# A transformer block's backward: nine buffers for the DMA-transposed ds tiles, two of their own for the one that TensorE transposes, six for the exps

## The chip, the cores and the metric

The kernel runs on one core of a Trainium2 chip. The metric is the device time of one execution in microseconds (us); the number that counts is the median over several executions. A profile is one execution, recorded instruction by instruction.

## What is computed

One transformer block with attention and a gated feed-forward network side by side, forward and backward in one launch. The sizes are S = 2048 tokens, D = 448, H = 16 heads of 28, F = 1792, all in bf16.

```python
def _fwd_reference(A_x, A_wqkv, A_wo, B_x, B_w_gate, B_w_up, B_w_down):
    ...
        scores = jnp.einsum("bhqd,bhkd->bhqk", q, k) * (Dh ** -0.5)
        p = _softmax(scores, axis=-1)
        o = jnp.einsum("bhqk,bhkd->bhqd", p, v)
        ...
        return (g * u) @ w_down
    x = A_x
    xn = _layernorm(x, axis=-1)
    return x + _A_ref(xn, A_wqkv, A_wo) + _B_ref(xn, B_w_gate, B_w_up, B_w_down)

def reference(A_x, A_wqkv, A_wo, B_w_gate, B_w_up, B_w_down, B_x, grad_out):
    ...
    _out, _vjp = jax.vjp(_f, A_x, A_wqkv, A_wo, B_w_gate, B_w_up, B_w_down)
    _grads = _vjp(grad_out)
    return (_out0, *[jnp.asarray(_g) for _g in _grads])
```

The outputs are the block's result and the gradients of the input and of the five weights.

## The kernel before

The order of all work is written out by hand; every engine runs its own list in that order, and waits are put in where a buffer or a value is not there yet. The first 610 us or so are the forward pass and the backward of the feed-forward network. What follows, up to some 1385 us, is the backward of attention, which the change touches; then a short end writes the gradient of the input.

**The loop.** The backward of attention runs 512 steps. A step is one tile of 512 keys by 128 queries for two heads; four steps with qi = 0, 1, 2, 3 are a block b of 512 queries, and there are 128 blocks. The list `steps` names the group of four heads (g), the head pair (hp), the chunk of keys (kc), the chunk of queries (qc) and qi of each step. Iteration k of the loop puts out:

- `row(k)`: on TensorE the scores of step k into PSUM banks named `sb` (L844, two heads) and the matrix that the softmax derivative needs for step k - 1 into banks named `db` (L852). Each name has three banks, and a bank holds one head, so `db` holds one and a half steps.
- `ew(k)`: on ScalarE the exponentials of step k out of `sb` into the SBUF tile `e_sb` (L868), and on VectorE ds of step k - 1 as the product of `db` and `e_sb` into the tile `ds_sb` (L874).
- For qi = 0, 1 and 2, straight after ds, a DMA transpose issued from SyncE (SP), which writes `ds_sb` transposed into the tile `dsT` of the block (L861, function `dst_dma`). Loads of later data (L801) stand in the same SP list, spread over the iterations by a planner (`drip` and `drop`).
- In iterations with k % 4 = 3, `tr_unit(b)` for b = (k - 7) / 4: the tile with qi = 3 is transposed by eight TensorE transposes (L929) and copied into `dsT` by ScalarE (L934). So the tile of step 4b + 3 is read here in iteration 4b + 7. In the very last block the tile with qi = 2 goes this way too.
- In iterations with k % 4 = 1, `kv` for the four steps of the last finished block, which reads `e_sb` (L947) and `ds_sb` (L951) on TensorE; block b is read in iteration 4b + 5. Then `dq_unit(b)` for b = (k - 13) / 4, which reads the block's whole `dsT` in sixteen matmuls (L978); block b is read in iteration 4b + 13.
- In the remaining places, pieces of other work on TensorE from a list (`stream`): the output of the feed-forward network (L1101), the gradient through gate and up (L1157) and more, each sized by the time there is.

**Buffers.** A tile name in a pool is a ring: with `bufs=8`, the ninth tile takes the place of the first and its first writer waits until all readers of that first tile are done. `ds_sb` has eight buffers and `e_sb` seven, 2 KB on each partition, in the pool `kq`. `dsT` has three, in the pool `bk`. The first three steps of the loop come before `bk` is opened; while `bk` is `None`, the transposes are kept in `pend` until it is.

**The end.** `dx_v` (L1298) and `dx_b` (L1337) take tiles of the rings `ds_sb` and `e_sb` for the last stage of the input's gradient.

Of the kernel before, what the change touches and what calls it, by code (L numbers as in the profile page):

```python
# [11 lines left out]
FP32 = mybir.dt.float32  # L12
BF16 = mybir.dt.bfloat16
# [4 lines left out]
D = 448  # L18
# [7 lines left out]
P = 128  # L26
# [79 lines left out]
def kernel(  # L106
# [465 lines left out]
    for i in range(len(chain) + LEAD):  # L572
# [4 lines left out]
        k = i - LEAD  # L577
# [117 lines left out]
    for c in range(3):  # L695
        k = 4 * c
        t = 4 * c + 4
# [35 lines left out]
    kq = None  # L733
# [87 lines left out]
    est, dss, sps, dps = {}, {}, {}, {}  # L821
# [34 lines left out]
    bk, pend = None, []  # L856

    def dst_dma(b, ds, qi):
        if qi == 0:
            dsT[b] = bk.tile([P, 4, 2, 4, P], BF16, name="dsT", bufs=3)  # L860
        SP.dma_start_transpose(out=dsT[b][:, qi].rearrange("p j kt s -> p (j kt) s"),  # L861
                               in_=ds[:].rearrange("p j k -> p (j k)"))

    def ew(k):
        if k < NB:
            est[k] = kq.tile([P, 2, 512], BF16, name="e_sb", bufs=7)
            for j in range(2):
                ACTE.activation(out=est[k][:, j], in_=sps.pop((k, j))[:], func=ACT.Exp, scale=SCALE)  # L868
        if 1 <= k <= NB:
            g, hp, kc, qc, qi = steps[k - 1]  # L870
            b = (k - 1) // 4
            ds = dss[k - 1] = kq.tile([P, 2, 512], BF16, name="ds_sb", bufs=8)
            for j in range(2):
                DVE.tensor_tensor(out=ds[:, j], in0=dps.pop((k - 1, j))[:], in1=est[k - 1][:, j], op=ALU.mult)  # L874
            if qi < 2 or qi == 2 and b < NB // 4 - 1:
                if bk is None:
                    pend.append(lambda: dst_dma(b, ds, qi))
                else:
                    dst_dma(b, ds, qi)
# [9 lines left out]
    k = n = 0  # L889
    for u in last[-5:]:  # L890
        for _ in u():
            n += 1
            if n in (8, 17, 25, 32):
                row(k)
                ew(k)
                k += 1
# [3 lines left out]
    bk = bwd.enter_context(tc.tile_pool(name="bk", bufs=2, reuse_waits="tile"))  # L900
# [393 lines left out]
    vs = {}  # L1294

    def dx_v(t):
        ps = psd.pop(t)
        vs[t] = kq.tile([P, 512], FP32, name="ds_sb", bufs=8)[:, :D]  # L1298
        dy = dy2[t // 4][:, t % 4, :] if t < 8 else dy4[:, t - 8, :]
        DVE.scalar_tensor_tensor(out=vs[t], in0=ps, scalar=rstd[:, t:t + 1], in1=dy, op0=ALU.mult, op1=ALU.add)  # L1300

    def sums(t, i):
        return sms[t - t % 2][:, i, t % 2:t % 2 + 1] if t < NT - 2 else sms[NT - 2 + i][:, t % 2:t % 2 + 1]
# [10 lines left out]
    def dx_a(t0):  # L1314
        for t in (t0, t0 + 1):
            ps = psd[t]
            sa, sb = sums(t, 0), sums(t, 1)
            if t not in EVEN:
                gs = dxs["tw"].tile([P, D], BF16, name="gs")
                ACTE.activation(out=gs[:], in_=ps, func=ACT.Identity, accum_out=sa)  # L1320
            else:
                psd[t] = dxs["g"][:, t, :]
                DVE.scalar_tensor_tensor(out=psd[t], in0=ps, scalar=1.0, in1=psd[t],
                                         op0=ALU.mult, op1=ALU.add, accum_out=sa)
            pr = dxs["tw"].tile([P, D], BF16, name="pr")
            DVE.scalar_tensor_tensor(out=pr[:], in0=psd[t], scalar=1.0, in1=xn_sp[:, t, :],
                                     op0=ALU.mult, op1=ALU.mult, accum_out=sb)
        if t0 == NT - 2:
            dx_sm(t0)
        for t in (t0, t0 + 1):  # L1330
            dx_v(t)
        if t0 < NT - 2:
            dx_sm(t0)

    def dx_b(t):
        sa, sb = sums(t, 0), sums(t, 1)
        u = kq.tile([P, 512], FP32, name="e_sb", bufs=7)[:, :D]  # L1337
        ACTE.activation(out=u, in_=xn_sp[:, t, :], func=ACT.Identity, scale=sb, bias=sa)  # L1338
        dx = dxs["tw"].tile([P, D], BF16, name="dx", bufs=4)
        (DVE if t == NT - 1 else POOL).tensor_tensor(out=dx[:], in0=u, in1=vs.pop(t), op=ALU.add)  # L1340
        SP.dma_start(out=out1_d[:, t, :], in_=dx[:])
# [3 lines left out]
    for k in range(NB + 12):  # L1345
        now = k
        if k < NB:
            g, hp, kc, qc, qi = steps[k]
# [7 lines left out]
        if k <= NB:  # L1356
            if k >= K0:
                row(k)
                ew(k)
            flush(k)  # L1360
            if 2 <= k:
                drop()
# [48 lines left out]
    for t in range(4, NT + 2, 2):  # L1411
        if t < NT:
            dx_mm(t)
            dx_a(t)
        for u in range(0 if t == 4 else t - 2, t):
            dx_b(u)
        for _ in range(at.get(t, 0)):
            run(rest.pop(0))
# [33 lines left out]
```

## Time and profile before

| | us |
|---|---|
| three runs | 1420.4, 1427.53, 1424.92 |
| their median | 1424.92 |
| the profiled execution | 1428.21 |
| its span, first to last instruction | 1426.4 |
| granted TensorE clock over the span | 0.974 of full |
| VectorE, L874: 1024 products of 684 ns, busy | 645.4 |
| ScalarE, L868: 1024 exponentials of 607 ns, busy | 541.7 |
| SP queue, hardware DMA: share of the 16 DMA engines | 88.6% |

The page gives the busy time of each engine, and the granted clock and the DMA load in 40 slices. A row of a group of instructions has its line, engine, operation, tiles and count, then busy time and the mean of one, then the idle time of the engine before them and what ended it. In a timeline the first two numbers are start and length, and the bracket holds the idle time before and its releaser. A list of waits has the total, the number of times and the longest, in us. A wait is put down to the engine that came last by the profile; now and then another name stands there than the one that was waited for.

### The profile page before, as it was taken

To read this page: it belongs to the slowest core of one execution; us is meant where nothing else is said; L and a number is where in the kernel's file an instruction comes from. 1 tells how busy PE (TensorE), PEld (TensorE's weight loads), DVE (VectorE), ACT (ScalarE), POOL (GpSimd) and SP (SyncE) were. 2 spreads that over 40 slices of the span, in tenths; PEclk is the share of its full clock that TensorE was granted. 3 is DMA by queue.
4 is the path that set the end of the run, shared out by engine and by line. 5 is a ranking of instruction groups with operands and counts; after the bars stand their busy time and mean duration, and the time that the engine had idled before them with its cause. 6 is when DMAs were issued, how large, how long until landed. Compare 5 with 4: busy or idle time off the path is not lost. (4 is left out here: it accounts for less than half of the span.)

```text
span 1426.4 us, 34639 instructions
## 1 busy us (share of the span) xinstructions
PE 1326.9 (93%) x12625; PEld 559.9 (39%) x12686; DVE 1149.3 (81%) x2001; ACT 1208.3 (85%) x2190; POOL 411.3 (29%) x577
## 2 busy tenths in 40 slices
PE   5899999999999999889999999999899999999995
PEld 2333333333333333334434434444344443444443
DVE  6677757666677676478989889988799998999988
ACT  5799988989999999768978779899789897888864
POOL 6574514454344454011211212201111112020105
PEclk9999999999999999989999999999999999999998
DMA  5797957796678686699999999999999999999982
GB/s 155 178 198 174 241 117 165 185 206 154 146 177 189 149 174 158 187 232 217 206 213 221 217 222 181 214 213 223 224 192 192 214 212 227 214 186 205 197 142 61
DMA packets 681692, 270.22 MB, mean 189 GB/s; under 512 B 607402, under 2 KB 656034, under 8 KB 681522
## 3 DMA queue, kind: packets, MB, share of 16 engines
q1 hardware_dynamic: 673074, 254.78, 88.6%
q0 software_dynamic: 7040, 12.93, 4.0%
q8 instruction: 99, 1.62, 0.5%
q14 instruction: 71, 0.58, 0.1%
q10 hardware_dynamic: 1408, 0.30, 0.1%
HBM read 64.37 MB, written 59.62 MB: 87 GB/s over the span
## 5 line engine op out<-in xcount | busy, mean ns | idle before, releaser
L874 DVE TENSOR_TENSOR ds_sb<-db,e_sb 128x512 bf16<-128x512 f32 x1024 | 645.4, 684 | 65.0 <-DMA dsT<-ds_sb 16.4
L868 ACT ACTIVATE e_sb<-sb 128x512 bf16<-128x512 f32 x1024 | 541.7, 607 | 55.4 <-PE db L852 45.4
L636 ACT ACTIVATE eT<-s_w 128x1024 bf16<-128x1024 f32 x256 | 264.6, 1033 | 54.2 <-PE s_ps L633 51.8
L638 ACT ACTIVATE eT<-s_ps 128x512 bf16<-128x512 f32 x512 | 287.2, 614 | 0.0
L852 PE MATMUL db<-kd,qd 32*128 32x512 bf16 x1024 | 239.6, 387 | 17.1 <-DVE ds_sb L874 16.6
L844 PE MATMUL sb<-kd,qd 32*128 32x512 bf16 x1024 | 232.9, 386 | 8.9 <-DMA qd<-QD_d 5.3
L993 POOL TENSOR_TENSOR dq_acc<-dq_acc,dq_st 128x256 f32<-128x256 f32 x64 | 46.2, 722 | 484.7 <-ACT dq_st L991 484.7
L404 POOL TENSOR_TENSOR nn<-nn,ag 128x512 f32<-128x512 f32 x56 | 71.2, 1271 | 242.2 <-DVE ag L402 233.5
L951 PE MATMUL acc<-ds_sb,qd 128*32 128x512 bf16 x1024 | 138.9, 393 | 0.2 <-DVE ds_sb L874 0.2
L947 PE MATMUL acc<-e_sb,qd 128*32 128x512 bf16 x1024 | 138.4, 393 | 0.0
L633 PE MATMUL s_ps<-QQ,KK 32*128 32x512 bf16 x512 | 120.3, 387 | 2.2
L1157 PE MATMUL genb<-wguT,dau_c 128*128 128x448 bf16 x448 | 110.5, 357 | 0.5 <-DMA dau_c<-F_d 0.5
L633 PE MATMUL s_w<-QQ,KK 32*128 32x512 bf16 x512 | 100.7, 389 | 3.6 <-ACT eT L636 1.2
L844 PEld LDWEIGHTS <-qd 32*128 32x128 bf16 x1024 | 48.5, 91 | 135.3 <-issue 114.7
L445 PE MATMUL gen<-xn_t,f_sp 128*128 128x448 bf16 x416 | 91.8, 354 | 3.2 <-DVE nn L419 1.9
L934 ACT COPY dsT<-sb 128x512 f32<-128x512 f32 x128 | 75.5, 590 | 18.1 <-PE sb L929 10.0
L445 PEld LDWEIGHTS <-f_sp 128*128 128x128 bf16 x640 | 55.7, 98 | 77.3 <-issue 32.3
L978 PE MATMUL sb<-dsT,kd 128*32 128x256 bf16 x2048 | 80.7, 279 | 0.7 <-ACT dsT L934 0.7
L929 PE MATMUL sb<-ident_bf,ds_sb 128*128 128x128 bf16 x1032 | 79.3, 220 | 1.0 <-DVE dsT L932 0.8
L929 PEld LDWEIGHTS <-ds_sb 128*128 128x128 bf16 x1032 | 67.7, 98 | 27.0 <-issue 8.3
L405 POOL TENSOR_TENSOR nn<-nn,tt 128x512 f32<-128x512 f32 x56 | 72.5, 1294 | 4.4
L475 PE MATMUL gen<-eT,VS 128*32 128x512 bf16 x1024 | 68.6, 383 | 5.3 <-ACT eT L638 2.2
(179 smaller groups left out, 1919.9 us busy)
## 6 DMA issues: line engine op xcount, KB each, us to landing
F_d<-hda SPq DMA_DIRECT2D x56, 384.0 KB
dau_c<-F_d SPq DMA_DIRECT2D x24, 512.0 KB
qd<-QD_d SPq DMA_DIRECT2D x16, 512.0 KB
kd<-KD_d SPq DMA_DIRECT2D x16, 384.0 KB
dsT<-ds_sb SPq DMA_TRANSPOSE x383
h_c<-F_d SPq DMA_DIRECT2D x8, 512.0 KB
wT_d<-wT_f SPq DMA_DIRECT2D x14, 256.0 KB
KD_d<-qk_sp SPq DMA_DIRECT2D x7, 512.0 KB
```

The costliest lines, as they stand in the source:

```text
L445: PE.matmul(ps[:, :D], lhsT=fsp[fc][:, t // 4, w, t % 4, :], rhs=rhs[:, t, :], start=(t == 0), stop=(t == NT - 1))
L633: PE.matmul(sp4[hh], lhsT=KK[g][r:r + HP, kt * P:(kt + 1) * P], rhs=QQ[g][r:r + HP, qsl], start=True, stop=True, tile_position=(r, 0))
L636: ACTE.activation(out=e2[0][:], in_=wide[:], func=ACT.Exp, scale=SCALE)
L638: ACTE.activation(out=e2[1][:, j], in_=sp4[2 + j], func=ACT.Exp, scale=SCALE)
L844: PE.matmul(s_ps[:], lhsT=qside[g, qc][r:r + HP, 0, qi * P:(qi + 1) * P], rhs=kside[g, kc][r:r + HP, 0, :], start=True, stop=True, tile_po ...
L852: PE.matmul(d_ps[:], lhsT=qside[g, qc][r:r + HP, 1, qi * P:(qi + 1) * P], rhs=kside[g, kc][r:r + HP, 1, :], start=True, stop=True, tile_po ...
L868: ACTE.activation(out=est[k][:, j], in_=sps.pop((k, j))[:], func=ACT.Exp, scale=SCALE)
L874: DVE.tensor_tensor(out=ds[:, j], in0=dps.pop((k - 1, j))[:], in1=est[k - 1][:, j], op=ALU.mult)
L929: PE.transpose(ps[:, c, :], ds[:, c // 4, (c % 4) * P:(c % 4 + 1) * P], ident_bf[:])
L947: PE.matmul(a[r:r + HP, :], lhsT=sp4[:, 1, r:r + HP], rhs=e[:, j, :], start=first, stop=last, tile_position=(0, r), skip_group_check=True)
L951: PE.matmul(a[r:r + HP, :], lhsT=sp4[:, 0, r:r + HP], rhs=ds[:, j, :], start=first, stop=last, tile_position=(0, r), skip_group_check=True)
L1157: PE.matmul(ps[:, :D], lhsT=d[:, i // 2, i % 2, tsl], rhs=dxs["w", fq][:, i // 2, i % 2, :], start=(i == 0), stop=(i == n - 1))
```

## The change

The tile of ds with qi = 3 no longer comes from the ring `ds_sb` but from a new ring `ds_pe` in the pool `bk`, which has two buffers, the pool's default. The ring `ds_sb` gets nine buffers instead of eight, the ring `e_sb` six instead of seven. So the pool `kq` has as much as before (15 tiles of these two names), and `bk` has two tiles of 2 KB on each partition more. The two other places where the rings are used (L1298 and L1337) have the new counts as well.

```diff
-            est[k] = kq.tile([P, 2, 512], BF16, name="e_sb", bufs=7)
+            est[k] = kq.tile([P, 2, 512], BF16, name="e_sb", bufs=6)
...
-            ds = dss[k - 1] = kq.tile([P, 2, 512], BF16, name="ds_sb", bufs=8)
+            by_pe = qi == 3 and bk is not None
+            ds = dss[k - 1] = (bk.tile([P, 2, 512], BF16, name="ds_pe") if by_pe else
+                               kq.tile([P, 2, 512], BF16, name="ds_sb", bufs=9))
...
-        vs[t] = kq.tile([P, 512], FP32, name="ds_sb", bufs=8)[:, :D]
+        vs[t] = kq.tile([P, 512], FP32, name="ds_sb", bufs=9)[:, :D]
...
-        u = kq.tile([P, 512], FP32, name="e_sb", bufs=7)[:, :D]
+        u = kq.tile([P, 512], FP32, name="e_sb", bufs=6)[:, :D]
```

## The prediction

> **What bounds the kernel now.** I read the page first (engines and slices), then stretches of the backward, the waits inside it, and the timeline around one wait. Columns of the stretches: start:end, length, busy time of PE, PEld, DVE, ACT and POOL, granted TensorE clock, mean share of the 16 DMA engines, GB/s.
>
> ```profile
> PE 1326.9 (93%) x12625; PEld 559.9 (39%) x12686; DVE 1149.3 (81%) x2001; ACT 1208.3 (85%) x2190; POOL 411.3 (29%) x577
> ```
> ```profile
> 720.00:750.00 30.00, 28.45 (x312) 11.69 (x311) 26.95 (x45) 22.83 (x46) 3.78 (x6) 0.94 1.20 209
> ...
> 780.00:815.00 35.00, 32.61 (x370) 14.15 (x372) 31.76 (x53) 29.20 (x59) 6.64 (x11) 0.97 1.13 215
> 815.00:835.00 20.00, 18.02 (x176) 7.22 (x169) 13.82 (x23) 12.44 (x26) 5.07 (x8) 0.80 1.12 238
> ...
> 850.00:880.00 30.00, 30.00 (x345) 13.32 (x342) 29.59 (x49) 27.69 (x56) 5.13 (x8) 1.00 1.02 187
> 1005.00:1025.00 20.00, 16.08 (x176) 6.33 (x174) 14.33 (x23) 12.57 (x26) 4.34 (x7) 0.91 1.09 221
> ...
> 1195.00:1215.00 20.00, 16.93 (x184) 6.99 (x183) 14.65 (x25) 12.84 (x27) 4.35 (x7) 0.91 1.10 221
> ```
>
> The backward (about 610 to 1385 us) is bound by TensorE: 850 to 880 shows PE at 30.00 of 30 us with full clock. Only in some stretches is PE idle, and there the clock falls too. The waits from 620 to 1385 us (us in total, times, longest) say behind whom:
>
> ```profile
> PE db L852 <- DVE ds_sb L874: 16.1, 19, 2.2
> ...
> DVE ds_sb L874 <- DMA dsT<-ds_sb: 16.4, 12, 3.5
> ```
>
> And one such wait, PE alone, SP alone, DVE alone:
>
> ```profile
> 717.94 0.39 PE L852 MATMUL db<-kd,qd 32*128 32x512 bf16 x1
> 720.49 0.55 PE L852 MATMUL db<-kd,qd 32*128 32x512 bf16 x1 [2.17 <-DVE ds_sb L874]
> ...
> 722.58 0.61 PE L844 MATMUL sb<-kd,qd 32*128 32x512 bf16 x2
> ```
> ```profile
> 712.53 5.59 SPq L861 DMA_TRANSPOSE dsT<-ds_sb  x2
> 718.16 0.60 SPq L801 DMA_DIRECT2D h_c<-F_d  x1
> 718.86 6.08 SPq L861 DMA_TRANSPOSE dsT<-ds_sb  x4
> ```
> ```profile
> 719.75 0.69 DVE L874 TENSOR_TENSOR ds_sb<-db,e_sb 128x512 bf16<-128x512 f32 x1 [2.59 <-DMA dsT<-ds_sb]
> ```
>
> The product ds (L874) cannot be written because the DMA transpose of the tile eight steps back has not landed. DVE stands for 2.59 us. The three db banks fill, PE stands for 2.17 us, and then its matmuls take 0.61 us instead of 0.39: the clock is at half for a while. SP has no hole: its transposes follow each other at 1.23 us or more.
>
> **What one such wait costs.** PE idle first. In the timeline of PE, the gaps of 0.4 us or more that end on L874 are 2.17, 1.06, 0.63, 0.63, 1.43, 1.98, 0.61, 2.22, 1.37, 1.56 and 0.40 us: 14.1 of the 16.1 us. Clock next, from the stretches above: (1 - 0.94) x 30 = 1.8, (1 - 0.97) x 35 = 1.0, 0.20 x 20 = 4.0, 0.09 x 20 = 1.8 twice: 10.4 us of full-speed time lost. What the transposes cost today is then 14.1 + 10.4 = 24.5 us.
>
> Here a rule speaks against half of that sum. The Trainium skill, page "TensorE: Matmul & The Clock Gate", section "Part 1: The HAM clock gate", has the clock fall after an idle window of about 3.4 us; no gap above is that long, so by the rule the 10.4 us would not belong to the waits, and the sum below would be -5.3 us instead of -12.3. The trace has the slow matmuls directly behind the 2.17 us gap, so I keep the 10.4 us.
>
> **The change part by part.**
>
> 1. Reuse distance of the transposed tiles. Before, all ds tiles go round eight buffers: step s waits for step s - 8. Now one in four (qi = 3) has other buffers and the rest go round nine: nine tiles are three blocks of four steps, so step s waits for step s - 12. A block takes about 5.7 us, so the DMA gets one block more. All waits on L874 for a DMA should go: -24.5 us, if nothing later is late.
>
> 2. What is late next. The same transpose is read by dq_unit(b) (L978), which PE reaches in iteration 4b + 13. Tile qi = 2 is reused before in iteration 4b + 11. The distance between the two in the trace: DVE freed at 719.75, 733.76, 751.13, 774.47, 798.18 us, dq_unit of that block at 724.40, 736.87, 754.25, 777.59, 801.29 us, so 4.6, 3.1, 3.1, 3.1, 3.1 us. So the margin is 3.1 us, not a whole block. SP issues without a hole, so a queue that is late stays late until a quieter stretch: I let waits that follow each other closely add up, take 3.1 us off each cluster, and put the rest on PE at L978. The DVE idle times that end with a landing (some carry another engine's name, which was done before; I went by the landing of the tile eight steps back): 0.76 + 2.59 + 1.43 = 4.8 (705 to 734 us), 0.67 + 1.01 + 0.45 + 1.01 + 1.31 + 2.36 = 6.8 (751 to 826), 0.88 + 1.21 + 0.63 = 2.7 (930 to 985), 0.55 + 2.30 + 1.77 = 4.6 (1007 to 1020), 0.65 (1123), 3.48 (1203). Rest: 1.7 + 3.7 + 0 + 1.5 + 0 + 0.4 = 7.3 us. Bounds: 0 (the margin and idle SP time suffice) and 23.1 us (the sum of all, nothing absorbed). I take 7.3, as the waits sit in clusters with quiet between. Behind a waiting dq_unit stands all of PE's queue, the next row (L844, L852) first, then ACT and DVE.
>
> 3. Clock after those waits. Gaps of 1.06 us and less left the clock alone, gaps of 1.4 and 2 us mostly did not. Two of the new waits may be that long: 2 x 1.7 us (half of a 3.4 us slow stretch, the length between 720.5 and 724) = 3.4 us. Bounds 0 and 10.4 us.
>
> 4. Loads. At 1200.5 us PE waits 1.5 us for qd and at 988 us 0.5 us for dau_c, both behind the same SP queue. With the loop faster they come no earlier: +1.5 us, between 0 and 4 (each twice).
>
> 5. ds of qi = 3 in two buffers of its own. Freed by kv in iteration 4b + 5 and by the transposes (L929) in 4b + 7, wanted again in 4b + 12: five iterations, 7 us, of cover. Cost 0. With the cover gone it would be the 0.6 us of the eight transposes once a block, 128 x 0.6 = 77 us.
>
> 6. e_sb six instead of seven. The exp of step k needs step k - 6 read by kv and by L874. kv of a block runs in iteration 4b + 5; the earliest exp that needs it is now in 4b + 6 instead of 4b + 7. But that exp reads an sb bank whose matmul (L844) stands behind this kv in PE's queue, so it waits no longer than it does anyway. L874 of step k - 6 is covered by the three db banks, which keep PE within two steps of DVE. Cost 0; bound below 0 excluded, above it one exp pair (2 x 607 ns) a block, which the order excludes.
>
> 7. Places in memory. kq keeps its size, bk grows by two tiles and pools behind it move. The order on PE, DVE, ACT, POOL and SP is the same instruction for instruction; only waits differ. New waits on forward work: the second exp tile waits for POOL L404 and DVE L431, which last started at 580.5 and 585.3 us, against the exp at 608.19 us. Cost 0.
>
> 8. The end: the 16 tiles of L1338 go round six instead of seven buffers behind POOL L1340 (1.2 us each). POOL waits for DVE there (31.2 us), so 0; bound +1.2 us, one L1340.
>
> Sum: -24.5 + 7.3 + 3.4 + 1.5 = -12.3 us. The profiled execution took 1428.2 us (span 1426.4 and 1.8 around it): 1415.9. It lies 3.3 us above the median of the runs shown, 1424.9; I carry the difference over: 1412.6, say **1412.5 us**.
>
> **The rivals.**
>
> *All of it is won.* If the queue recovers between waits, items 2 to 4 are 0: 1424.9 - 24.5 = 1400.4 us. For it: single waits at 1123 and 1203 us are far apart. Against: SP without a hole at 706 to 725 us. Chance 0.15.
>
> *The queue is the bound.* DMA share 1.02 to 1.20 in all stretches. If the transposes come at the DMA engines' pace, all 23.1 us come back at L978, less clock loss: -24.5 + 23.1 = about 1424 us. Against: 850 to 880 us, where the DMA is as full and PE never waits. The profile's page counts 607402 of 681692 DMA packets under 512 B. Chance 0.28. The Trainium skill, page "DMA: Bandwidth & Descriptors", section "Specifications", puts the least transfer for line rate at 512 B; by it these transposes are bound by their packets, and a buffer more would win nothing.
>
> *Slower: the wait lands where it costs most.* A late ds is softened by 1.5 steps of db banks; a late dsT stops PE at once, at L978, and each stop over 1.3 us may cost a slow stretch. With all 23.1 us there and as many slow stretches as waits over 0.6 us (15 x 1.7 = 25): -24.5 + 48 = +24, 1449 us. It decides once waits plus clock at L978 pass 24.5 us. Against: the margin of 3.1 us. Chance 0.12.
>
> *It does not do what it says*: the ring of eight never held DVE, the named releaser being wrong. Then 1425 us. Against: the 2.59 us wait has nothing else to end it. Chance 0.03.
>
> **How the numbers follow.** The forecast has 0.42, its own range 1405 to 1420 us. What a measurement of this kernel can tell from no change is about 0.5%, 7 us. Faster: 0.36 of the forecast's 0.42, 0.15, and 0.05 of the queue case = 0.56. Same: 0.06 + 0.21 + 0.03 = 0.30. Slower: 0.12, and 0.02 of the queue case = 0.14. The range 1400 to 1432 us leaves out most of the slower case and some of the fullest win.
>
> **What would show it.** After: no "DVE ds_sb L874 <- DMA dsT" in the waits (item 1), a new wait of L978 for the DMA of dsT of some 7 us (item 2), granted clock 1.00 at 1005 to 1025 and 1195 to 1215 us or their like, PE's wait for L874 down from 16.1 to a few us. ACT e_sb L868 waiting for PE acc L947 would prove item 6 wrong. If L978 waits more than 20 us for the DMA, the queue was the bound and the forecast is wrong.

## The result and the profile after

The changed kernel takes 1417.45 us (median of eight runs, 1409.88 to 1419.96) against 1425.47 us for the one before (eight runs): ratio 0.9935, 95% interval 0.991 to 0.996, so 8 us less. It was measured beside its kernel before in two more sessions: 0.9944 (0.9923 to 0.9964) and 0.9898 (0.9876 to 0.9920). The profiled execution took 1417.71 us, its span is 1415.9 us. Lines below the edit have moved by two: the ds product is L876, `dq_unit`'s matmuls are L980.

The engines on the page of the changed kernel, first TensorE's row:

```profile
PE 1326.4 (94%) x12686; PEld 558.6 (39%) x12686; DVE 1147.4 (81%) x2001; ACT 1208.5 (85%) x2190; POOL 411.1 (29%) x577
```

The busy times are those of before; the span is 10.5 us shorter, and its mean granted clock is 0.978 against 0.974. The stretches of the changed kernel (columns as before):

```profile
720.00:750.00 30.00, 30.00 (x350) 13.21 (x351) 29.53 (x50) 27.64 (x56) 3.78 (x6) 1.00 1.22 198
780.00:815.00 35.00, 34.15 (x401) 14.80 (x389) 33.92 (x57) 30.97 (x62) 7.35 (x12) 1.00 1.17 223
815.00:835.00 20.00, 14.47 (x154) 5.72 (x155) 12.35 (x21) 11.60 (x24) 4.35 (x7) 0.91 1.15 239
850.00:880.00 30.00, 29.86 (x364) 13.29 (x353) 29.27 (x49) 27.28 (x56) 5.14 (x9) 1.00 1.11 202
1005.00:1025.00 20.00, 18.33 (x208) 8.00 (x206) 17.33 (x29) 17.22 (x36) 3.22 (x5) 1.00 1.15 234
1185.00:1205.00 20.00, 17.25 (x189) 7.21 (x187) 15.31 (x27) 13.46 (x28) 4.52 (x8) 0.91 1.15 225
```

At 720 to 750 us PE is now busy throughout, with full clock; before it lost 1.55 us idle and 1.8 us to the clock there. Two of these stretches are still bad, at 815 and at 1185 us. The list of PE's waits from 620 to 1385 us in the changed kernel (us in total, times, longest) says what fills them:

```profile
PE sb L980 <- DMA dsT<-ds_sb: 4.9, 4, 2.7
PE sb L844 <- DMA qd<-QD_d: 4.4, 2, 2.7
...
PE sb L844 <- DMA kd<-KD_d: 1.9, 1, 1.9
PE db L852 <- DVE ds_sb L876: 1.4, 5, 0.5
...
PE genb L1159 <- DMA dau_c<-F_d: 0.3, 1, 0.3
```

PE's wait for the ds product fell from 16.1 to 1.4 us, and the DVE's wait for the DMA of dsT is gone from the list altogether. In its place PE waits 4.9 us for dsT itself, at `dq_unit`, and 6.3 us for loads of qd and kd. All four waits for dsT lie between 773 and 825 us. The longest of them and the wait for kd behind it, then the granted clock (third number from the end) in the stretch between the two and right after the second:

```profile
817.27 0.62 PE L980 MATMUL sb<-dsT,kd 128*32 128x256 bf16 x16 [2.67 <-DMA dsT<-ds_sb]
...
829.41 0.61 PE L844 MATMUL sb<-kd,qd 32*128 32x512 bf16 x2 [1.90 <-DMA kd<-KD_d]
```
```profile
816.00:829.00 13.00, 8.88 (x102) 3.86 (x102) 7.98 (x13) 7.96 (x16) 4.35 (x7) 1.00 1.17 248
829.00:833.00 4.00, 3.59 (x24) 1.05 (x28) 2.59 (x5) 1.89 (x4) 0.00 (x0) 0.57 1.13 209
```

How one of the loads comes late, SP first, then PE:

```profile
1183.84 4.02 SPq L861 DMA_TRANSPOSE dsT<-ds_sb  x2
1187.91 1.31 SPq L801 DMA_DIRECT2D qd<-QD_d  x1
1189.31 3.99 SPq L861 DMA_TRANSPOSE dsT<-ds_sb  x2
```
```profile
1193.41 0.39 PE L844 MATMUL sb<-kd,qd 32*128 32x512 bf16 x2 [2.73 <-DMA qd<-QD_d]
```

The load is issued at 1187.91 us between transposes, PE is ready for it at 1190.68 us, and it is there at 1193.41 us.

### The profile page after: what moved, and what is told of

Same layout as the page of the kernel before. It is cut to its first block, busy times and chain, and to the rows that moved or that the text cites. A ratio compares the mean times of both kernels' runs of the same rounds, so it can differ in the third digit from the quotient of the medians.

```text
span 1415.9 us, 34707 instructions
## 1 busy us (share of the span) xinstructions
PE 1326.4 (94%) x12686; PEld 558.6 (39%) x12686; DVE 1147.4 (81%) x2001; ACT 1208.5 (85%) x2190; POOL 411.1 (29%) x577
## 5 line engine op out<-in xcount | busy, mean ns | idle before, releaser
L876 DVE TENSOR_TENSOR ds_sb<-db,e_sb 128x512 bf16<-128x512 f32 x768 | 482.0, 683 | 36.4 <-issue 13.8
L852 PE MATMUL db<-kd,qd 32*128 32x512 bf16 x1024 | 234.1, 385 | 2.9 <-DVE ds_sb L876 1.4
L876 DVE TENSOR_TENSOR ds_pe<-db,e_sb 128x512 bf16<-128x512 f32 x256 | 164.8, 686 | 19.2 <-PE db L852 10.9
L953 PE MATMUL acc<-ds_sb,qd 128*32 128x512 bf16 x768 | 108.4, 391 | 0.0
L980 PE MATMUL sb<-dsT,kd 128*32 128x256 bf16 x2048 | 80.1, 277 | 5.7 <-DMA dsT<-ds_sb 4.9
L931 PE MATMUL sb<-ident_bf,ds_pe 128*128 128x128 bf16 x1024 | 78.6, 220 | 1.0 <-DVE dsT L934 0.8
L931 PEld LDWEIGHTS <-ds_pe 128*128 128x128 bf16 x1024 | 67.3, 98 | 26.9 <-issue 8.2
```

The source lines that it names most:

```text
L852: PE.matmul(d_ps[:], lhsT=qside[g, qc][r:r + HP, 1, qi * P:(qi + 1) * P], rhs=kside[g, kc][r:r + HP, 1, :], start=True, stop=True, tile_po ...
L931: PE.transpose(ps[:, c, :], ds[:, c // 4, (c % 4) * P:(c % 4 + 1) * P], ident_bf[:])
L953: PE.matmul(a[r:r + HP, :], lhsT=sp4[:, 0, r:r + HP], rhs=ds[:, j, :], start=first, stop=last, tile_position=(0, r), skip_group_check=True)
```

## The experiments

The first three tell apart what brought the 8 us; the others ask what bounds the rest. All are compared with the kernel before on their own chip.

**Six ds_sb buffers: the distance undone, all else kept.**

```diff
-                               kq.tile([P, 2, 512], BF16, name="ds_sb", bufs=9))
+                               kq.tile([P, 2, 512], BF16, name="ds_sb", bufs=6))
```

> The changed kernel with six ds_sb buffers instead of nine: a transposed tile is reused after 8 steps again, ds_pe and the six exps stay. If the reuse distance is what brought the 8 us, the time goes back to that of before, about 1425 us, with DVE waiting at the ds product for the DMA of dsT some 15 to 25 us again. If it was that the tile of qi = 3 has buffers of its own (its place, or its leaving the ring), the time stays at about 1417 us.

Measured: 1427.11 us, ratio 1.0004 (0.998 to 1.0028). Two waits of its backward, the first on PE, the second on DVE:

```profile
PE db L852 <- DVE ds_sb L876: 16.8, 20, 2.5
```
```profile
DVE ds_sb L876 <- DMA dsT<-ds_sb: 16.4, 12, 2.7
```

Both are back at what they were before (16.1 and 16.4 us), and the whole gain is gone, although the tile of qi = 3 still has buffers of its own. So it is the reuse distance of the transposed tiles that the change lives from; the two own buffers and the six exps bring nothing without it, they make room for it.

**Eight ds_sb buffers: ten or eleven steps.**

```diff
-                               kq.tile([P, 2, 512], BF16, name="ds_sb", bufs=9))
+                               kq.tile([P, 2, 512], BF16, name="ds_sb", bufs=8))
```

> The changed kernel with eight ds_sb buffers instead of nine: the distance is 10 or 11 steps. A tile of qi = 2 would then be reused in iteration 4b + 14, after dq_unit has read its transpose in 4b + 13. If dq_unit is the next thing that a late transpose holds, the ninth buffer does nothing: 1417 us, no wait of DVE for the DMA. If the time follows the number of buffers, it lies between, about 1420 us.

Measured: 1418.56 us, ratio 0.9933 (0.9914 to 0.9953), the same as with nine. PE's and then DVE's list:

```profile
PE sb L980 <- DMA dsT<-ds_sb: 4.8, 6, 1.4
PE sb L844 <- DMA qd<-QD_d: 4.8, 2, 2.4
```
```profile
DVE ds_sb L876 <- DMA dsT<-ds_sb: 3.8, 4, 1.8
```

DVE still waits four times, 3.8 us, which the expectation did not have: the tile of qi = 0 is then reused ten steps later, in iteration 4b + 11, before `dq_unit`. No cost of it shows, and no gain of the ninth buffer; the step from 8 to 10 or 11 brings all that these intervals, some 0.2% to either side, can tell.

**Six exps, nothing else.** The kernel before with `e_sb` at six:

```diff
-            est[k] = kq.tile([P, 2, 512], BF16, name="e_sb", bufs=7)
+            est[k] = kq.tile([P, 2, 512], BF16, name="e_sb", bufs=6)
```

> The kernel before with six exps instead of seven and nothing else. If the sixth-back exp is always read before TensorE can fill the next score bank, the time is that of before, 1425 us within 0.3%, and the exps never wait for kv. If the shorter ring costs something that the net of 8 us hides, the time is some 3 us or more above before, 1428 us and more, with ScalarE waiting for kv.

Measured: 1427.7 us, ratio 0.9996 (0.9978 to 1.0013). ScalarE's longest wait in its backward is the one of before (42.8 us, 57 times), and no wait of the exps for kv is in the list:

```profile
ACT e_sb L868 <- PE db L852: 39.9, 58, 3.6
```

The shorter ring is free.

**The qd loads earlier.** The changed kernel, due times of qd moved by eight steps:

```diff
-        drip(("q", g, qc), [(t[:], QD_d[g, qc])], 128 * g + 4 * qc - 4)
+        drip(("q", g, qc), [(t[:], QD_d[g, qc])], 128 * g + 4 * qc - 12)
```

> The changed kernel with the loads of qd due eight steps (some 11 us) earlier. In the changed kernel PE waits 1.90, 1.67 and 2.73 us for qd at three of the turns between head groups, and one slow stretch of 1.7 us of lost clock follows. If these loads are only issued too late, the gaps go: about -6 to -8 us against the changed kernel, 1410 us. If the queue is full anyway and an earlier load only makes the transposes around it later, the waits move to dq_unit and the time stays at 1417 us.

The wait of 1.90 us in this expectation is for kd, not for qd, as PE's list above has it.

Measured: 1414.77 us, ratio 0.9915 (0.9893 to 0.9937). No wait for qd is left, but PE's list now has

```profile
PE sb L980 <- DMA dsT<-ds_sb: 9.4, 7, 4.4
...
PE sb L844 <- DMA kd<-KD_d: 0.7, 1, 0.7
```

instead of 4.9 us for dsT and 6.3 us for qd and kd. By these two traces PE waits 5.6 us less for the loads and 4.5 us more for the transposes beside them. The intervals of this kernel and of the changed one overlap, so a gain is not shown.

**qd and kd earlier**, with the changed kernel a third time beside it. The edit is the one above and the same eight steps for kd (`- 12` for `- 4`).

> The changed kernel a third time, as the one that the next is compared with on the same chip: ratio to before 0.994 within 0.3%.

> The changed kernel with the loads of qd and of kd due eight steps earlier. The changed kernel waits 4 to 6 us of PE time for late qd and kd loads. If late issue is all, these waits go and nothing comes in their place: 6 us under the changed kernel, ratio to before 0.990. If the DMA engines are full, about half of it comes back as wait for dsT at dq_unit, as with qd alone: 2 to 4 us under the changed kernel, ratio 0.992. If the earlier loads push the transposes further back than they help, no gain, 0.994.

Measured: the changed kernel 1414.06 us, ratio 0.9898 (0.9876 to 0.9920); with both loads early 1420.94 us, ratio 0.9934 (0.9910 to 0.9958). PE's lists, first the changed kernel measured beside it, then with both loads early:

```profile
PE sb L980 <- DMA dsT<-ds_sb: 6.5, 5, 3.9
PE sb L844 <- DMA qd<-QD_d: 4.4, 2, 2.5
```
```profile
PE sb L980 <- DMA dsT<-ds_sb: 11.8, 10, 3.0
```

The second list has neither qd nor kd; the first has kd with another 0.5 us. The third outcome came: of 4.9 us of waits for qd and kd none is left, and 5.3 us more are waited at `dq_unit`. The waits move between users of the DMA; their sum does not fall. The time is 6.9 us above the changed kernel beside it, with intervals that overlap a little; the lists of waits do not show where all of it comes from.

**The loads on another queue.** The changed kernel again as control, and with the planner's loads issued by POOL:

```diff
             _, _, o, i = slow.pop(0)
-            SP.dma_start(out=o, in_=i)
+            POOL.dma_start(out=o, in_=i)
```

> The changed kernel once more, beside the next three, so that they are compared with it on the same chip: ratio to before 0.9935 within 0.3%.

> The changed kernel with the planner's loads (those that drop issues) on the POOL queue instead of SP, so that SP issues transposes and forced loads alone. If SP's one-after-the-other issue is what makes the transposes late, the wait of PE for dsT at dq_unit and for qd (4.9 and 4.4 us in the changed kernel) goes and the time falls by 6 to 9 us, to about 1410 us. If it is the 16 DMA engines that are full, the same packets come over another queue and nothing is won: 1417 us or more, with dq_acc on POOL behind waiting loads.

Measured: the control 1419.31 us, ratio 0.9944 (0.9923 to 0.9964); with the loads on POOL 1483.05 us (median of six, 1465.52 to 1497.09), ratio 1.036 (1.0314 to 1.0407) without the two longest. Of the latter, from a profiled execution of 1488.27 us, a stretch, a wait of PE and SP's transposes in that stretch, and below them SP's timeline of the changed kernel in the same 30 us:

```profile
850.00:880.00 30.00, 16.79 (x190) 7.36 (x189) 15.83 (x27) 14.35 (x30) 1.08 (x2) 0.77 1.17 146
```
```profile
PE sb L980 <- DMA dsT<-ds_sb: 70.1, 20, 13.2
```
```profile
845.92 34.67 SPq L861 DMA_TRANSPOSE dsT<-ds_sb  x11
```
```profile
849.74 3.03 SPq L861 DMA_TRANSPOSE dsT<-ds_sb  x2
852.83 0.58 SPq L801 DMA_DIRECT2D kd<-KD_d  x1
853.50 26.48 SPq L861 DMA_TRANSPOSE dsT<-ds_sb  x17
```

SP has almost nothing but transposes to issue now, and eleven of them take 34.67 us, 3.15 us each, where the changed kernel's seventeen take 26.48 us, 1.56 us each. So loads between the transposes in SP's queue are not what makes them late; loads beside them, from another queue, are worse. The DMA share in this stretch is 1.17 with 146 GB/s, against 1.02 and 187 before with a single load in it. That the engines are full, or that the other queue's loads are served first, both fit. So does the size of the packets: by the packet counts of the two pages the loads that moved, some 49 MB, are 33570 packets on SP's queue and 13744 on POOL's. Which of the three it is was not tried.

**dq_unit one iteration later.** The changed kernel, `dq_unit(b)` moved from iteration 4b + 13 to 4b + 14, ahead of the piece of other work there; then the same with the early qd loads.

```diff
-            b = (k - 13) // 4
-            if 0 <= b < NB // 4:
-                dq_unit(b)
...
         elif m == 2:
+            b = (k - 14) // 4
+            if 0 <= b < NB // 4:
+                dq_unit(b)
             if 9 <= k < NB:
```

> The changed kernel with dq_unit one iteration later (4b + 14 instead of 4b + 13), the same three dsT buffers. The margin of the transposes at dq_unit grows by a step, 1.4 us. If late transposes there are what is left of the cost, PE's wait of 4.9 us falls to about 2 us and the time by 2 to 4 us, to about 1414 us; the waits for qd stay. If freeing dsT a step later delays SP's transposes (SP stands some 4 us behind), or its sb bank collides with tr_unit, the time rises to 1420 us or more.

> Both: qd loads eight steps earlier and dq_unit one iteration later. With the loads early the changed kernel loses its waits for qd and waits more at dq_unit (9.4 us); one step more of margin should take off about 1.4 us of each of those seven waits. If so: 1409 to 1411 us, 3 to 5 us under the early loads alone. If the waits only move on, 1414 us.

Measured: 1436.8 us, ratio 1.0072 (1.0044 to 1.0099), and 1435.24 us, ratio 1.0059 (1.0038 to 1.0081). In neither list does PE wait for dsT any more, so the margin is what that wait hangs on, as expected. But a block has become longer, where no DMA is waited for too: with `dq_unit` alone moved, the first kv matmuls of two blocks stand 6.07 us apart in a quiet stretch (1336.37 and 1342.44 us), against 5.55 us in the changed kernel (lines below). So a third edit put the piece of other work of 560 ns into `dq_unit`'s old place, again with and without early loads:

```diff
         elif m == 1:
...
-            b = (k - 13) // 4
-            if 0 <= b < NB // 4:
-                dq_unit(b)
+            if 9 <= k < NB:
+                if cur is None:
+                    fill_open(BIG)
+                fill_step(R2)
...
         elif m == 2:
-            if 9 <= k < NB:
-                if cur is None:
-                    fill_open(BIG)
-                fill_step(R2)
+            b = (k - 14) // 4
+            if 0 <= b < NB // 4:
+                dq_unit(b)
```

> The changed kernel with dq_unit in iteration 4b + 14 as in the run before, and the piece of other TensorE work that stood there (560 ns) put into 4b + 13 in its stead, so that the rows of score matmuls keep their spacing. If the 17 us that the later dq_unit lost came from uneven spacing (two rows with kv alone between them), the block is back to 5.55 us in a quiet stretch, the wait of PE for dsT is gone, and the time is 1408 to 1412 us. If they came from dq_unit no longer following kv at once, the block stays at about 6 us and the time at 1436 us.

> The same, with the loads of qd eight steps earlier. If spacing was it, both waits of PE for a DMA (dsT and qd) are gone and the time is 1404 to 1409 us, under both kernels; if not, 1435 us.

Measured: 1448.47 us, ratio 1.0145 (1.0109 to 1.0182), and 1447.85 us, ratio 1.0137 (1.0102 to 1.0171). Equal spacing did not bring the block back. PE's timeline in a quiet stretch, first the changed kernel (the first kv matmuls of two blocks that follow each other), then the swap:

```profile
1336.38 0.39 PE L949 MATMUL acc<-e_sb,qd 128*32 128x512 bf16 x2
...
1341.93 0.39 PE L949 MATMUL acc<-e_sb,qd 128*32 128x512 bf16 x2
```
```profile
1335.04 0.39 PE L949 MATMUL acc<-e_sb,qd 128*32 128x512 bf16 x2
...
1337.02 0.62 PE L980 MATMUL sb<-dsT,kd 128*32 128x256 bf16 x16
1337.77 0.86 PE L844 MATMUL sb<-kd,qd 32*128 32x512 bf16 x2
...
1341.12 0.39 PE L949 MATMUL acc<-e_sb,qd 128*32 128x512 bf16 x2
```

A block takes 5.55 us in the one and 6.08 us in the other. In every block that would be 128 x 0.53 = 68 us; 29 to 34 us are in the time, since the changed kernel's blocks are longer elsewhere: from the first score matmul of the loop to the last it takes 758.7 us, the swap 791.3 us, 0.25 us more a block. What stands out is the score pair behind `dq_unit`: 0.86 us, where the one behind it takes 0.39 us in the changed kernel (1337.79 us). `dq_unit` takes one of the three sb banks, and in its new place the next row comes after 0.75 us, before ScalarE has emptied a second one. That it is the bank is argued from these lines, not tested; that this place is worse whether work stands around it or not is measured.

## Why the prediction was right, point by point

The forecast was 1412.5 us, faster, from 1400 to 1432; measured are 1417.45 us. The terms against the profiled pair:

| step | predicted | measured |
|---|---|---|
| 1. waits and slow clock behind the 8-step reuse | -24.5 | gone but for 1.4 us of PE's 16.1; back with six buffers |
| 2. wait at `dq_unit` instead | +7.3 | +4.9 |
| 3. slow clock behind those waits | +3.4 | 0.09 x 20 us twice, +3.6, but behind loads |
| 4. later loads | +1.5 | qd 4.4, kd 1.9 and dau_c 0.3 against qd 1.5 and dau_c 0.5 before: +4.6 |
| sum | -12.3 | -24.5 + 4.9 + 3.6 + 4.6 = -11.4 |

The mechanism of items 1 and 2 was right: the waits behind the short reuse distance go, and part of them comes back at `dq_unit`. But the clusters of item 2 fitted in one place only. From 751 to 826 us it forecast 3.7 us, and all 4.9 us came there; at 705 to 734, 1007 to 1020 and 1203 us it forecast 3.6 us, and none came. Near two of these places PE waits for qd instead, 1.67 us at 1012 us and 2.73 us at 1193 us.

Item 4, "With the loop faster they come no earlier: +1.5 us", is the term that was mis-sized: 4.6 us, above its upper bound of 4. It is the same queue seen from the other side, as the runs with early loads show, and items 2 and 4 should have been one term: together 8.8 us were forecast and 9.5 us came. The two other traces of the changed kernel have 9.1 and 11.4 us for dsT, qd and kd, the profiled one above 11.2, so the sum is steadier than its parts.

Item 3 hit its number by luck. It expected slow clock behind waits for dsT, but the longest of these, 2.67 us, left the clock at 1.00; the two slow stretches stand directly behind waits for loads, kd at 829 us and qd at 1193 us. The same mistake is in item 1: the slow stretch at 1205 us before, 1.8 us of its 10.4, stood behind a wait for qd as well as one for ds, and it came back behind qd alone. The two waits before:

```profile
1202.02 0.39 PE L844 MATMUL sb<-kd,qd 32*128 32x512 bf16 x2 [1.52 <-DMA qd<-QD_d]
...
1203.97 0.37 PE L852 MATMUL db<-kd,qd 32*128 32x512 bf16 x1 [1.55 <-DVE ds_sb L874]
```

The profiled execution fell by 10.5 us, 0.9 us less than the sum. The loop itself fell by 11.7 us: its score matmuls run from 606.0 to 1376.4 us before and from 608.1 to 1366.8 us after. So it started 2 us later, ahead of anything the change touches in it. The medians fell by 8.0 us, since the execution profiled before lay 2.7 us above its median of eight and the one after 0.3 us above its own; the prediction had carried 3.3 us over to both.

Items 5 to 8, each costed at nothing: six exps are shown to be free by the run with that edit alone. Two buffers for qi = 3 cost nothing that shows: in DVE's list for the changed kernel the product into `ds_pe` waits for db and for ScalarE, never for the transposes on TensorE or for kv, which read it. The places in memory and the shorter ring at the end were not tried alone; they are inside the run with six buffers, which is level with before.

The rivals. "All of it is won" is out: 9.5 us of waits came back. "The queue is the bound" holds in half: what the loop no longer waits for at the ds product comes back in part as waits for dsT and loads, and whoever is served earlier takes it from the other; but most of the 23.1 us did not come back at `dq_unit`, as the margin of 3.1 us and the quiet stretches would have it. The argument against it from 850 to 880 us was weak, since 1.02 is the lowest DMA share of the rows shown. "Slower" needed a slow stretch behind nearly every wait at `dq_unit`; directly behind those four there was none. "It does not do what it says" is ruled out by the run with six buffers.

## What to carry to other kernels

A ring of buffers whose readers are DMAs is judged by its distance in steps against the landing time, and tiles with a quick reader should not take turns in it: taking one tile in four out of the ring, and one buffer from the exps, bought a whole block of distance for 4 KB more on each partition. Before adding a buffer, look for the next reader of the same late value, since its margin, here 3.1 us and not the block of 5.7, is what can be won; what goes beyond it moves there. And where the DMA engines are nearly full, as here, moving transfers earlier only changed who waits, and moving them to another queue made the waits longer; look at the sum of all waits for DMAs, not at one.

## What was not expected of the hardware

Ordinary loads on the POOL queue slowed the transposes on SP far more than the same loads between them on SP: PE's waits for dsT went from 4.9 us to 70.1 us, the longest 13.2 us.

And idle gaps of PE far shorter than the 3.4 us of the Trainium skill's page "TensorE: Matmul & The Clock Gate" (section "Part 1: The HAM clock gate") stood ahead of slow clock in the changed kernel too. The granted clock is 0.91 over 1185 to 1205 us with one gap of 2.73 us, while at 1005 to 1025 us, with a gap of 1.67 us, it stayed at 1.00. The length of the gap does not decide it either: behind 2.67 us at 817 us the clock stayed at 1.00, behind 1.90 us at 829 us it was 0.57 for 4 us. And from 650 to 680 us the clock is low before (first line) and after, though PE has no gap of more than 0.24 us there in either trace:

```profile
650.00:680.00 30.00, 28.38 (x294) 10.96 (x290) 25.23 (x42) 24.70 (x52) 3.62 (x6) 0.89 1.12 218
```
```profile
650.00:680.00 30.00, 28.34 (x283) 10.61 (x280) 23.57 (x40) 23.11 (x49) 3.97 (x6) 0.83 1.12 220
```

The change leaves this stretch alone; what slows it was not tried.
